# Thresholded attention with a feed-forward block: quarter products added up in their accumulator banks, T2 in the centred tokens' room, and weights turned in place

## Chip, core and metric

The kernel runs on one core of a Trainium2 chip. The metric is the device time of one execution in microseconds (us), as the median of several runs. Engines are named as in the profile: PE is TensorE (matmul), PEld its weight load, DVE VectorE, ACT ScalarE, POOL GpSimd, SP the queue that issues most transfers.

## What is computed

Two stages, all in fp32. First, attention with a threshold for 8 batches of 8 heads, 576 tokens, 64 features per head: scores below their row's maximum less tau are dropped before the softmax. The heads are put side by side to 576 tokens of 512 features. Second, a feed-forward block on them: normalise each token, multiply by w_ch1 (512 x 2048), take the positive part, multiply by w_ch2 (2048 x 512), add the tokens.

```
scores = q @ k.T / 8
scores = where(scores >= rowmax(scores) - tau, scores, -1e9)
a = exp(scores - rowmax);  a = a / (sum(a) + 1e-9);  x = a @ v      # 8 heads -> (8, 576, 512)
xn = (x - mean(x)) / sqrt(var(x) + 1e-6) * g_ln
out = x + maximum(xn @ w_ch1, 0) @ w_ch2
```

## The kernel before

**Attention in slots.** A batch is cut into 9 slots: four pairs of heads with the first 256 queries, one slot with the last 64 queries of all four pairs, and four pairs with the queries 256 to 511. There are 72 slots, n = 0 to 71. In each slot:

- PE writes the scores into two PSUM rooms (L422).
- `exponentials(n)`: DVE takes the negated row maximum (L436), POOL makes the threshold `thr` from it (L440), ACT writes the exponentials into a room `e` in SBUF (L449), four blocks of 128 x 576.
- `weights`: DVE compares with the threshold and masks each block, with its row sum (L458), and takes the reciprocal of each pair of sums (L463). POOL multiplies each block by its reciprocal, "the division" (L474), two blocks as soon as a reciprocal is there.
- `turn_blocks` (from slot n = 6 on): DVE transposes blocks of 32 x 32 out of `e` into a tile `et` (L548, and L542 for the slot with the last queries). SP sends `et` to a room `scr` in DRAM (L555, L559), and fetches it back as `em` and `er` with the keys along the partitions (L569 to L578). So the weights are transposed by a way through DRAM, one slot later.
- `values_of`, two slots later: PE multiplies `em` and `er` by the values (L617, L627), into the same PSUM rooms, and ACT copies the result into the tokens x (L640, L635).

New q and k come by transfer, POOL scales q (L355), and DVE transposes both (kT L373, qT L377 and L382, q_last L383).

**Feed-forward in groups.** The tokens of a batch make two groups of 288, so there are 16 groups, g = 0 to 15. POOL sums the features (L669), PE makes the mean from the sum, DVE centres the tokens into a room `xc` (L692). `first_part(g)` has 64 products of 128 x 288, whose positive parts ACT writes into the room `hidden` (L834). The variance's root comes out as `rb`. The second part of group 0 is plain. From group 1 on, `second_quarters` multiplies by w_ch2 as 2 x 2 blocks with seven products of quarters in place of eight. Each product is a *segment*: 16 calls of `product`, which are 32 matmuls of 64 columns (two records each in the profile). A segment accumulates in one of the two PSUM banks `ff`, in turn, and ACT copies it out (L912). b11, b12, b21 and b22 are the quarters of `hidden` (first or second half of the features; `early` or `late` half of the tokens). Besides segments there are sums of quarters, two halves of 128 x 576 each (L897):

- T3 = b22 - b12 (POOL, into b12); T2 = b11 + T3 (DVE, into b11); T4 = b21 - T2 (POOL, into b21); T1 = b22 - T2 (DVE, into b11)
- S2, S3, S4: differences of weight quarters, made once in group 1
- segments in order: w00·b11, w01·b21, s3·T3, s2·T2, w11·T4, w10·T1, s4·b22
- seven additions of 128 x 2 x 144 of their copies (L937), named u2, 11, u3, 21, 22, u4 and 12; then `finish` multiplies by `rb` (L945) and adds x (L937), and `store` transposes the result into `ot` (L737), which goes to the output.

**What sets the order.** Each engine runs its instructions in the order in which the program emits them; a tile framework adds the waits. The program emits slot by slot, each slot in four quarters. In every quarter `second_part(n, i)` takes steps from the generator of the group at hand, as many products as a share by hand (`ROOM`) says, so that PE always has products between the steps of the attention. The sums of quarters and the additions are not emitted where the generator comes by them: `later` puts them into a list `drops`, with an engine and a cost. Calls of `drip` in the loop over the slots take them from it (the ones marked `urgent` at the next call); `need` emits all of the list up to the ones named, at once. So the place of a sum among the instructions of its engine follows from the quarter in which the generator passed it. After a slot's first quarter those urgent for POOL at the head of the list are emitted as well.

```
def need(*what):
    while not done.issuperset(what):
        drops.pop(0)[-1]()
```

**Weights.** w_ch1 and w_ch2 arrive as raw 64-bit words and are converted in 32 chunks during the first slots, in rooms that are free then (`Weights`: ACT L295 and L300, DVE L310 to L317, POOL L325). One of them is the tile `et`, another is the second `e` room, which after slot 6 is free and later holds S4.

Of the kernel before, what the change touches and what calls it, by code (L numbers as in the profile page):

```python
# [18 lines left out]
def kernel(  # L19
# [87 lines left out]
    hidden = consts.tile([128, ND, TOK], F32, name="hidden")  # L107
    e_room = [consts.tile([128, 4, S], F32, name=f"e{i}") for i in range(2)]

# [84 lines left out]
    class Weights:  # L194
# [13 lines left out]
        def __init__(self):  # L208
# [21 lines left out]
            y_room = ffn.tile([128, NK, TOK], F32, tag="sq", bufs=1, name="y_room")  # L230
            et_room = att.tile([128, NB, 128], F32, tag="et", bufs=1, name="et_room")
            stage = self.stage = consts.tile([128, 8, WC], F32, name="stage")
# [6 lines left out]
            for t, n, before in (  # L239
                (w2_sb.rearrange("p m d c -> p (m d) c"), ND // 2, lambda p: (16, 16, 19, 21, 24, 24, 25, 29)[p]),  # L240
                (hidden, 4, lambda p: 10),
                (x_room, 1, lambda p: 2 * n1),
                (y_room, 1, lambda p: 2 * n1),
                (et_room, 2, lambda p: n1 - 3),
                (stage, 4, lambda p: 2 * n1),
            ):
                for p in range(n):
                    home = 99 if t.shape[-1] != 128 or n != ND // 2 else n1 + 2 * p
                    self.free.append(
                        (before(p), -1, flat(t)[:, p * 2 * WC : (p + 1) * 2 * WC], home)  # L250
                    )

        def take(self, t):
            t = t.rearrange("p a b -> p (a b)")
            for p in range(2):
                self.free.append((2 * self.n1, -1, t[:, p * 2 * WC : (p + 1) * 2 * WC], 99))

# [102 lines left out]
    def turn(u):  # L360
# [7 lines left out]
        if not 0 < u < HP:  # L368
            scale_q(u, q_in)
        qT = att.tile([128, 2, QH], F32, tag="qT", bufs=4, name="qT")  # L370
        kT = att.tile([128, S], F32, tag="kT", bufs=4, name="kT")
        ql = q_last[u % HP]
        nc.vector.transpose(kT, k_in.rearrange("p n c -> p (n c)"))  # L373
        for s in range(2):
            part = q_in[:, 9 * s : 9 * s + 8]
            if by_blocks(units[u][0] * SLOTS + units[u][1] + (HP + 1 if s else 0)):
                nc.vector.transpose(  # L377
                    qT[:, s].rearrange("p (j a c) -> p a j c", j=2, a=4),
                    part.rearrange("p (a j) c -> p a j c", j=2),
                )  # L380
            else:
                nc.vector.transpose(qT[:, s], part.rearrange("p n c -> p (n c)"))  # L382
        nc.vector.transpose(  # L383
# [21 lines left out]
    def scores(b, s):  # L405
# [12 lines left out]
        for t, h, j, at, n, o in sorted(pieces):  # L418
            r = slice(64 * h, 64 * h + 64)
            for i in range(2):  # L420
                qT, kT, ql = turned[b * HP + (2 * j + i if s == HP else hp)]
                nc.tensor.matmul(  # L422
                    sc[h][64 * i : 64 * i + 64, at : at + n],
                    lhsT=ql[r] if s == HP else qT[r, half, j * 128 + 64 * i : j * 128 + 64 * i + 64],
                    rhs=kT[r, o : o + n], start=True, stop=True,
                )

    def exponentials(n):
# [3 lines left out]
        thr = small.tile([128, 4], F32, tag="thr", name="thr")  # L432
        es = e_room[(n + 1) % 2 if n <= FIRST else 0]
        for h in range(2):
# [11 lines left out]
        for i in range(4):  # L446
            if i == 2:
                yield es, thr
            nc.scalar.activation(es[:, i], blocks[i], func=AF.Exp, bias=neg[:, i : i + 1])  # L449

    def weights(n, es, thr, divide):
# [3 lines left out]
        for i in range(4):  # L455
            if i == 3:
                run(n, "mask")
            nc.vector.scalar_tensor_tensor(  # L458
                out=es[:, i], in0=blocks[i], scalar=thr[:, i : i + 1], in1=es[:, i],
                op0=ALU.is_ge, op1=ALU.mult, accum_out=den[:, i : i + 1],  # L460
# [75 lines left out]

    def turn_blocks(b, s, es):


        et = att.tile([128, NB, 128], F32, tag="et", bufs=1, name="et")  # L540
        if s == HP:
            nc.vector.transpose(  # L542
                et.rearrange("p n (u c) -> p u n c", u=HP),
                es.rearrange("p u (n c) -> p u n c", c=32),
            )
        else:
            for h in range(2):
                nc.vector.transpose(  # L548
                    et[:, :, 64 * h : 64 * h + 64].rearrange("p n (j c) -> p j n c", j=2),
                    es[:, 2 * h : 2 * h + 2].rearrange("p j (n c) -> p j n c", c=32),  # L550
                )
        scr = dram.tile([4, S, 128], F32, tag="scr", name="scr")
        if b == 0:
# [6 lines left out]
            out=scr.rearrange("a (r n) x -> (a r) (n x)", r=32),  # L560
            in_=et.rearrange("p n x -> p (n x)"),
        )
# [212 lines left out]
    def differences():  # L775


        flat = conversion.stage.rearrange("p a b -> p (a b)")
        flat4 = e_room[1].rearrange("p a b -> p (a b)")
        size = HM * HD * 128  # L780
        for t in (flat[:, :size], flat[:, size : 2 * size], flat4[:, :size]):
            more.append(t.rearrange("p (m d c) -> p m d c", m=HM, d=HD))
        s2, s3, s4 = more
        s1 = w2[1, 0]
# [12 lines left out]
    def first_part(g):  # L797
# [6 lines left out]
        for d in range(ND):  # L804
# [6 lines left out]
            for c in range(NK):  # L811
# [4 lines left out]
                if c == NK // 2 - 1 and sq is not None and rb is None and (  # L816
# [8 lines left out]
                    if plain:  # L825
                        two = [ffn.tile([128, HM, HT], F32, tag="part", bufs=4, name="two") for _ in two]
                        two = [t.rearrange("p m t -> p (m t)") for t in two]
                    nc.scalar.activation(two[0], var, func=AF.Identity, bias=eps_sb)
# [38 lines left out]
    def second_quarters(g, rb):  # L867
# [9 lines left out]
        part_of = lambda t, i, j: t[:, HM * i : HM * i + HM, (early, late)[j]]  # L877
        y11, y12, y21, y22 = (part_of(y, i, j) for i in range(2) for j in range(2))
        done = set()

# [17 lines left out]

        def segment(weights, rhs, out=None):
            seg = bank(HM, HT)  # L900
            for d in range(HD):
                for m in range(HM):
                    at, end = (d, m), (HD - 1, HM - 1)
                    product(
                        seg[:, m], lhsT=weights[:, m, d], rhs=rhs[:, d],
                        start=at == (0, 0), stop=at == end,
                    )
                    if at != end:
                        yield 2, 0.5
            if out is None:  # L910
                out = ffn.tile([128, HM, HT], F32, tag="part", bufs=4, name="part")
            nc.scalar.copy(out, seg)  # L912
            return out

        def last_tiles(weights, rhs):


            for m in range(HM):
# [8 lines left out]
                drip(everything=True)  # L927
                z = ffn.tile([128, HT], F32, tag="part", bufs=4, name="z")
                dve.tensor_tensor(out=z, in0=end, in1=rb[:, late], op=ALU.mult)
# [9 lines left out]
        def finish(eng, i, j=None):  # L939
# [11 lines left out]
        banks_taken[0] = True  # L951
        yield from segment(w2[0, 0], b11, y11)
        need("t3")
        later(("t2", 3, by_fours, dve, b11, b11, b12, ALU.add), urgent=dve)
        yield 2, 0.5
        p2 = yield from segment(w2[0, 1], b21)
        need("t2")
        later(("t4", 3, by_fours, pool, b21, b21, b11, ALU.subtract), urgent=pool)
        yield 2, 0.5
        p7 = yield from segment(s3, b12)  # L960
        yield 2, 0.5
        yield from segment(s2, b11, y12)
        need("t4")
        later(("t1", 3, by_fours, dve, b11, b22, b11, ALU.subtract), urgent=dve)
        later(
            ("u2", 1, add, pool, y12, y12, y11), ("11", 1, add, pool, y11, y11, p2),
            ("done11", 2, finish, pool, 0, 0),
        )
        yield 2, 0.5
        p4 = yield from segment(w2[1, 1], b21)  # L970
        later(("u3", 1, add, dve, y22, y12, p7), ("21", 1, add, dve, y21, y22, p4))
        if ends_here:
            later(("done21", 2, finish, dve, 1, 0))
        yield 2, 0.5
        need("t1", "u2", "11")
        p5 = yield from segment(w2[1, 0], b11)
        later(("22", 1, add, dve, y22, y22, p5), ("u4", 1, add, dve, y12, y12, p5))
        if ends_here:
# [6 lines left out]
        yield 2, 0.5  # L985
        last = last_tiles(s4, b22) if ends_here else segment(s4, b22)
        for _ in range(12 if g % 2 == 0 else 8):
            yield next(last)
        banks_taken[0] = False
        while waiting_mean:  # L990
            mean_of(waiting_mean.pop(0))
        p3 = yield from last
        if not ends_here:
            later(
                ("12", 1, add, dve, y12, y12, p3), ("done12", 2, finish, pool, 0, 1),
                *((f"o{m}", 1, store, dve, g, m, y[:, m]) for m in (2, 3, 0, 1)),
            )
# [116 lines left out]
    for n in range(NS):  # L1114
# [10 lines left out]
        rest = exponentials(n)  # L1125
        es, thr = next(rest)
        conversion.carry_all()
# [44 lines left out]
        if blocks_go:  # L1172
            conversion.fetch(0 if n == FIRST + 2 else 3, wait=0)
            conversion.prepare_to(end_at, False)
            scr = turn_blocks(b, s, es)
            if n == FIRST:
                conversion.take(e_room[1])
            if n == FIRST:
# [83 lines left out]
```

## Time and profile before

| | us |
|---|---|
| median of 3 runs | 1339.2 (1338.88 to 1339.34) |
| the profiled execution, its own time | 1339.53 |
| its span in the profile | 1337.5 (2.03 lie around it) |
| one batch (two groups, nine slots) in the steady part | 157.28 |
| one segment of 64 records, 128 x 144 | 3.92 |
| L458 mask, DVE, mean of one | 0.810 |
| L474 division, POOL, median and mean of one | 0.747, 0.794 |
| L897 sum of quarters, half of it: POOL mean, DVE mean | 1.426, 0.886 |
| L937 addition: DVE, POOL, median of one with two y operands | 0.457, 0.803 |
| L912 copy, ACT | 0.404 |
| L548 transposes of 1152 elements, DVE, mean of one | 1.376 |
| L542 transposes of 2304 elements, DVE, mean of one | 2.58 |
| scr from et, from issue to landing, median | 5.0 |
| em from scr, from issue to landing, median | 5.7 |

The profile shows one execution. Times in it count from the start of the span. A line of a timeline gives the start, the busy time (of all instances, where it has an x count), engine, source line, operation, the tile written <- those read, shapes, and in brackets how long the engine idled before and what released it. A matmul is "busy" from its issue to a modelled end, so that PE's time says when it had work, not how well it used its array. TensorE's granted clock was 0.998 of full speed.

PE idled before a matmul for 20 us in all in the list of waits; 5.6 of them (3 waits) were for POOL's conversion of weights (L325), 2.6 for the centred tokens, 2.0 for one transfer of em. All but 0.6 us of these end before 180 us, or stand behind 1260 us.

### The profile page before, as it was taken

To read this page: it belongs to the slowest core of one execution; us is meant where nothing else is said; L and a number is where in the kernel's file an instruction comes from. 1 tells how busy PE (TensorE), PEld (TensorE's weight loads), DVE (VectorE), ACT (ScalarE), POOL (GpSimd) and SP (SyncE) were. 2 spreads that over 40 slices of the span, in tenths; PEclk is the share of its full clock that TensorE was granted. 3 is DMA by queue.
4 is the path that set the end of the run, shared out by engine and by line. 5 is a ranking of instruction groups with operands and counts; after the bars stand their busy time and mean duration, and the time that the engine had idled before them with its cause. 6 is when DMAs were issued, how large, how long until landed. Compare 5 with 4: busy or idle time off the path is not lost.

```text
span 1337.5 us, 40245 instructions
## 1 busy us (share of the span) xinstructions
PE 1310.3 (98%) x17304; PEld 996.2 (74%) x17304; DVE 872.5 (65%) x1544; ACT 457.7 (34%) x995; POOL 624.7 (47%) x836
## 2 busy tenths in 40 slices
PE   8899899999999999999999999999999999999997
PEld 7665567769687786968778696877869687786967
DVE  7879886667666675666756677566756667666113
ACT  5866323232423233232233324233232323333120
POOL 3475556535445444445535454443444445345312
PEclk9999999999999999999999999999999999999999
DMA  8946874457543775447734676447754376443211
GB/s 160 293 119 174 206 190 156 179 154 196 176 151 128 191 197 162 152 157 200 191 127 151 171 180 192 139 143 198 196 171 153 133 191 179 139 149 141 73 19 20
DMA packets 335298, 213.92 MB, mean 160 GB/s; under 512 B 247376, under 2 KB 292688, under 8 KB 327056
## 3 DMA queue, kind: packets, MB, share of 16 engines
q1 hardware_dynamic: 329008, 210.46, 54.0%
q8 instruction: 136, 2.23, 0.7%
q10 hardware_dynamic: 5952, 0.74, 0.4%
q0 software_dynamic: 160, 0.15, 0.1%
q14 instruction: 42, 0.34, 0.1%
HBM read 124.00 MB, written 87.29 MB: 158 GB/s over the span
## 4 chain that ended last, share of the span: by engine, by line
PE 91%; ACT 2%; DVE 2%; SPq 2%; DMA 1%; POOL 1%; issue 1%; POOLq 0%; DVEq 0%; ACTq 0%
PE ff L118 70%; PE sc L422 10%; PE sc L617 9%; PE sc L627 2%; SPq L135 1%; ACT e L449 1%; POOL w L325 1%; DVE e L458 1%; DVE xc L692 0%; DMA v_in<-in_v_dram 0%; DVE neg L436 0%; DMA k_in<-in_k_dram 0%; DMA scr<-et 0%; DMA qk_room<-in_k_dram 0%; POOL e L474 0%
## 5 line engine op out<-in xcount | busy, mean ns | idle before, releaser
L118 PE MATMUL ff<-xc,w 128*64 128x288 f32 x4096 | 516.5, 407 | 2.8 <-DVE xc L692 2.0
L118 PEld LDWEIGHTS ff<-xc,w 128*64 128x64 f32 x4096 | 293.5, 137 | 199.9 <-issue 13.9
L436 DVE TENSOR_REDUCE neg<-sc 128x2 f32<-128x1152 f32 x144 | 188.7, 1352 | 269.3 <-PE sc L422 268.7
L118 PE MATMUL ff<-hidden,w 128*64 128x144 f32 (+1 forms) x4096 | 281.2, 294 | 5.7 <-POOL w L325 5.6
L118 PEld LDWEIGHTS ff<-hidden,w 128*64 128x64 f32 x4096 | 252.7, 137 | 31.0 <-issue 9.6
L474 POOL TENSOR_SCALAR e<-e,den 128x576 f32<-128x576 f32 x264 | 206.3, 794 | 141.2 <-DVE den L463 141.2
L458 DVE SCALAR_TENSOR_TENSOR e<-sc,thr,e 128x576 f32<-128x576 f32 x288 | 222.9, 810 | 19.3 <-POOL thr L440 11.7
L440 POOL TENSOR_SCALAR thr<-neg,low_sb 128x2 f32<-128x2 f32 x144 | 39.7, 277 | 378.2 <-DVE neg L436 377.5
L834 ACT ACTIVATE hidden<-ff 128x288 f32<-128x288 f32 x256 | 106.8, 417 | 282.8 <-PE ff L118 278.9
L449 ACT ACTIVATE e<-sc,neg 128x576 f32<-128x576 f32 x288 | 197.8, 754 | 2.6 <-DVE neg L436 2.6
L548 DVE STREAM_TRANSPOSE et<-e 128x1152 f32<-128x1152 f32 x118 | 162.0, 1376 | 16.5 <-POOL e L474 15.9
L422 PE MATMUL sc<-kT,qT 64*64 64x384 f32 (+3 forms) x2048 | 140.2, 403 | 2.0 <-DVE e L458 1.6
L617 PE MATMUL sc<-em,v_in 128*64 128x128 f32 (+1 forms) x2368 | 131.6, 265 | 2.3 <-DMA em<-scr 2.0
L617 PEld LDWEIGHTS sc<-em,v_in 128*64 128x64 f32 x2368 | 124.6, 138 | 10.7 <-DVE den L463 2.2
L118 PE MATMUL ff<-hidden,stage 128*64 128x144 f32 x1920 | 123.3, 286 | 0.0
L118 PEld LDWEIGHTS ff<-hidden,stage 128*64 128x64 f32 x1920 | 117.6, 137 | 2.9 <-issue 2.9
L640 ACT COPY x<-sc 128x128 f32<-128x128 f32 x120 | 31.8, 266 | 245.4 <-PE sc L422 175.7
L897 POOL TENSOR_TENSOR hidden<-hidden 128x576 f32<-128x576 f32 x60 | 84.7, 1426 | 51.7 <-ACT hidden L834 42.1
L422 PEld LDWEIGHTS sc<-kT,qT 64*64 64x64 f32 x2048 | 76.3, 133 | 43.5 <-issue 21.4
L912 ACT COPY part<-ff 128x288 f32<-128x288 f32 x74 | 29.9, 404 | 191.2 <-PE ff L118 190.8
L897 DVE TENSOR_TENSOR hidden<-hidden 128x576 f32<-128x576 f32 x60 | 51.1, 886 | 49.6 <-PE ff L118 46.7
L118 PE MATMUL ff<-hidden,e 128*64 128x144 f32 x960 | 65.5, 286 | 0.0
(126 smaller groups left out, 988.9 us busy)
## 6 DMA issues: line engine op xcount, KB each, us to landing
scr<-et SPq DMA_DIRECT2D x63, 1152.0 KB, 5.0
em<-scr SPq DMA_DIRECT2D x63, 1024.0 KB, 5.7
out_dram<-ot SPq DMA_DIRECT2D x248, 36.0 KB, 3.9
q_in<-in_q_dram SPq DMA_DIRECT2D x120, 72.0 KB, 2.6
er<-scr SPq DMA_DIRECT2D x132, 64.0 KB, 5.1
k_in<-in_k_dram SPq DMA_DIRECT2D x116, 72.0 KB, 2.9
v_in<-in_v_dram SPq DMA_DIRECT2D x28, 256.0 KB, 5.4
w<-in_moe_w_ch_dram SPq DMA_DIRECT2D x10, 512.0 KB, 8.0
```

The lines of the kernel that those rows point to most:

```text
L118: nc.tensor.matmul(out[r], lhsT=lhsT[:, r], rhs=rhs, **flags)
L422: nc.tensor.matmul(sc[h][64 * i : 64 * i + 64, at : at + n], lhsT=ql[r] if s == HP else qT[r, half, j * 128 + 64 * i : j * 128 + 64 * i + 64],
L436: nc.vector.tensor_reduce(out=neg[:, i], in_=pairs[h], axis=AXL.X, op=ALU.max, negate=True,)
L440: nc.gpsimd.tensor_scalar(out=thr[:, i], in0=neg[:, i], scalar1=-1.0, scalar2=low_sb, op0=ALU.mult, op1=ALU.add,)
L449: nc.scalar.activation(es[:, i], blocks[i], func=AF.Exp, bias=neg[:, i : i + 1])
L458: nc.vector.scalar_tensor_tensor(out=es[:, i], in0=blocks[i], scalar=thr[:, i : i + 1], in1=es[:, i], op0=ALU.is_ge, op1=ALU.mult, accum_o ...
L474: nc.gpsimd.tensor_scalar(out=es[:, i], in0=es[:, i], scalar1=den[:, i : i + 1], scalar2=1.0, op0=ALU.mult, op1=ALU.mult,)
L548: nc.vector.transpose(et[:, :, 64 * h : 64 * h + 64].rearrange("p n (j c) -> p j n c", j=2), es[:, 2 * h : 2 * h + 2].rearrange("p j (n c) ...
L617: nc.tensor.matmul(dst[64 * h : 64 * h + 64], lhsT=vt[:, h, c, :], rhs=pick(em[:, 2 * j : 2 * j + 2, c], h), start=c == 0 and first, stop= ...
L640: nc.scalar.copy(x_of(2 * b + (s > HP))[:, s % (HP + 1), 128 * j : 128 * j + 128], pv[j])
L834: nc.scalar.activation(hidden[:, d], p1, func=AF.Relu)
L897: eng.tensor_tensor(out=out[at], in0=in0[at], in1=in1[at], op=op)
```

## The change

The list of segments is put in another order, and products that belong to one result are accumulated on top of each other in a bank, which ACT copies out in between:

- segment 1 is w01·b21, copied to y12; segment 2 is w00·b11 in a bank `one`, copied to y11; segment 3 is s3·T3 in the bank `two`, copied to y22; segment 4 adds s2·T2 into `one`, copied to y21; segment 5 adds w11·T4 into `two`, copied into a part of T2's tile; segment 6 adds w10·T1 into `one`, copied to y12; segment 7 is s4·b22, copied to a tile `rest`.
- The additions 11, 21, 22 and 12 are left; u2, u3 and u4 go.
- T2 has a tile of its own, in the ring of the centred tokens (tag "xc", one room). T1 is still written into b11, T4 into b21.
- T4 waits for T2 by `need` after segment 3; before, after segment 2.
- The tiles `part` go; `rest`, z and two small tiles of group 0 take the tag "o".
- `et` goes. The weights are written with the four blocks interleaved in runs of 32 columns ("p (n i c)"), where they are turned by blocks, and DVE transposes them where they lie, in two calls in every slot. SP sends `scr` from the room itself. Both `e` rooms are used in turn in all slots.
- S4 has a tile of its own, which also stages weights; `et` and the second `e` room do so no longer. qT is split into two tiles, one for each half of the queries (2 and 4 rooms).

```diff
-    e_room = [consts.tile([128, 4, S], F32, name=f"e{i}") for i in range(2)]
+    e_room = [consts.tile([128, 4 * S], F32, name=f"e{i}") for i in range(2)]
+    s4_room = consts.tile([128, NK // 2, ND // 2, 128], F32, name="s4")
+    def by_rows(e):
+        return e.rearrange("p (i s) -> p i s", i=4)
+    def by_columns(e):
+        return e.rearrange("p (n i c) -> p i n c", i=4, c=32)
...
-                (et_room, 2, lambda p: n1 - 3),
+                (s4_room.rearrange("p m d c -> p (m d) c"), 2, lambda p: 2 * n1),
...
-        qT = att.tile([128, 2, QH], F32, tag="qT", bufs=4, name="qT")
+        qT = [att.tile([128, QH], F32, tag=f"qT{i}", bufs=2 + 2 * i, name=f"qT{i}") for i in range(2)]
...
+    def as_in(es, block):
+        return block if len(es.shape) == 3 else block.rearrange("p (n c) -> p n c", c=32)
...
-        es = e_room[(n + 1) % 2 if n <= FIRST else 0]
+        room = e_room[(n + 1) % 2]
+        es = by_columns(room) if by_blocks(n) else by_rows(room)
...
-            nc.scalar.activation(es[:, i], blocks[i], func=AF.Exp, bias=neg[:, i : i + 1])
+            nc.scalar.activation(
+                es[:, i], as_in(es, blocks[i]), func=AF.Exp, bias=neg[:, i : i + 1]
+            )
...
-    def turn_blocks(b, s, es):
-        et = att.tile([128, NB, 128], F32, tag="et", bufs=1, name="et")
-        if s == HP:
-            nc.vector.transpose(
-                et.rearrange("p n (u c) -> p u n c", u=HP),
-                es.rearrange("p u (n c) -> p u n c", c=32),
-            )
-        else:
-            for h in range(2):
-                nc.vector.transpose(
-                    et[:, :, 64 * h : 64 * h + 64].rearrange("p n (j c) -> p j n c", j=2),
-                    es[:, 2 * h : 2 * h + 2].rearrange("p j (n c) -> p j n c", c=32),
-                )
+    def turn_blocks(b, s, room):
+        et = room.rearrange("p (n x) -> p n x", x=128)
+        for h in range(2):
+            two = et[:, :, 64 * h : 64 * h + 64]
+            nc.vector.transpose(two, two)
...
-            in_=et.rearrange("p n x -> p (n x)"),
+            in_=room,
...
+        t2 = ffn.tile([128, NK, TOK], F32, tag="xc", bufs=1, name="t2")
+        t2 = t2.rearrange("p c t -> p (c t)").rearrange("p (d t) -> p d t", d=HD)
...
-        def segment(weights, rhs, out=None):
-            seg = bank(HM, HT)
+        def segment(weights, rhs, out, seg=None):
+            more_of_it = seg is not None
+            if not more_of_it:
+                seg = bank(HM, HT)
...
-                        start=at == (0, 0), stop=at == end,
+                        start=at == (0, 0) and not more_of_it, stop=at == end,
+                        skip_group_check=more_of_it,
...
-            return out
+            return seg
...
-        yield from segment(w2[0, 0], b11, y11)
+        yield from segment(w2[0, 1], b21, y12)
+        later(("t2", 3, by_fours, dve, t2, b11, b12, ALU.add), urgent=dve)
+        yield 2, 0.5
+        one = yield from segment(w2[0, 0], b11, y11)
         need("t3")
-        later(("t2", 3, by_fours, dve, b11, b11, b12, ALU.add), urgent=dve)
         yield 2, 0.5
-        p2 = yield from segment(w2[0, 1], b21)
+        two = yield from segment(s3, b12, y22)
         need("t2")
-        later(("t4", 3, by_fours, pool, b21, b21, b11, ALU.subtract), urgent=pool)
+        later(("t4", 3, by_fours, pool, b21, b21, t2, ALU.subtract), urgent=pool)
+        later(("11", 1, add, pool, y11, y11, y12), ("done11", 2, finish, pool, 0, 0))
         yield 2, 0.5
-        p7 = yield from segment(s3, b12)
+        yield from segment(s2, t2, y21, one)
+        need("t4")
+        later(("t1", 3, by_fours, dve, b11, b22, t2, ALU.subtract), urgent=dve)
         yield 2, 0.5
-        yield from segment(s2, b11, y12)
-        need("t4")
-        later(("t1", 3, by_fours, dve, b11, b22, b11, ALU.subtract), urgent=dve)
-        later(
-            ("u2", 1, add, pool, y12, y12, y11), ("11", 1, add, pool, y11, y11, p2),
-            ("done11", 2, finish, pool, 0, 0),
-        )
-        yield 2, 0.5
-        p4 = yield from segment(w2[1, 1], b21)
-        later(("u3", 1, add, dve, y22, y12, p7), ("21", 1, add, dve, y21, y22, p4))
+        need("t1", "11")
+        yield from segment(w2[1, 1], b21, t2[:, :HM], two)
+        later(("21", 1, add, dve, y21, y21, t2[:, :HM]))
...
-        need("t1", "u2", "11")
-        p5 = yield from segment(w2[1, 0], b11)
-        later(("22", 1, add, dve, y22, y22, p5), ("u4", 1, add, dve, y12, y12, p5))
+        yield from segment(w2[1, 0], b11, y12, one)
+        later(("22", 1, add, dve, y22, y22, y12))
...
-        last = last_tiles(s4, b22) if ends_here else segment(s4, b22)
+        need("21")
+        next_bank(two)
+        rest = ffn.tile([128, HM, HT], F32, tag="o", bufs=4, name="rest")
+        last = last_tiles(s4, b22) if ends_here else segment(s4, b22, rest)
...
-            scr = turn_blocks(b, s, es)
-            if n == FIRST:
-                conversion.take(e_room[1])
+            scr = turn_blocks(b, s, room)
```

## The prediction

> **What bounds the kernel now.** First the page's busy table: it says which engine fills the span.
>
> ```profile
> PE 1310.3 (98%) x17304; PEld 996.2 (74%) x17304; DVE 872.5 (65%) x1544; ACT 457.7 (34%) x995; POOL 624.7 (47%) x836
> ```
>
> TensorE (PE) is busy in 1310.3 of 1337.5 us. The 27.2 us left are not spread out: 20-us windows show 19 us of it before 180 us (while the weights are converted), 0.6 near 254 us, 0.7 near 1270 us and 7.4 us behind PE's last matmul. In between PE never pauses:
>
> ```profile
> 160.00:180.00 20.00, 17.82 (x184) 10.99 (x178) 17.19 (x33) 6.48 (x13) 10.29 (x13) 1.00 0.71 179
> 380.00:400.00 20.00, 20.00 (x368) 18.83 (x364) 13.47 (x19) 4.17 (x9) 10.12 (x13) 1.00 0.52 186
> 537.00:557.00 20.00, 20.00 (x362) 18.83 (x360) 13.75 (x19) 4.17 (x9) 10.40 (x13) 1.00 0.53 182
> 1200.00:1220.00 20.00, 20.00 (x206) 12.89 (x204) 12.77 (x22) 8.26 (x18) 12.04 (x16) 1.00 0.31 120
> ```
>
> (The second number is PE's busy time; the next are its weight loads, DVE, ACT and POOL.) So work taken off DVE, ACT or POOL there gains nothing, while any operand that is late for PE is paid in full: nothing later wins it back. PE's own work is unchanged: the changed program holds the same matmuls in the same interleaving. The forecast is thus a search for operands that come late.
>
> **The late one: T4 in the odd groups.** The second part of a group has seven segments of 32 matmuls (64 records, 3.92 us). Fifth is w11·T4. Before, T4 (POOL, two halves) was emitted ahead of segment 3, two segments before its use. Now it waits for T2 and is emitted behind segment 3, one segment before its use. POOL runs in order, so I laid POOL's list of the changed program beside that of before. In even groups T4 stays behind the slot's four divisions. In groups 3, 5, 7, 9, 11 and 13 it stood ahead of them (thr, sum, thr, T4, four divisions) and now stands behind them. In group 1 it stays ahead. The timeline of before, group 3, PE then POOL then DVE:
>
> ```profile
> 543.93 8.01 PE L118 MATMUL ff<-hidden,stage 128*64 128x144 f32 x128
> 551.77 1.52 PE L118 MATMUL ff<-hidden,w 128*64 128x144 f32 x22
> ```
>
> ```profile
> 546.45 2.81 POOL L897 TENSOR_TENSOR hidden<-hidden 128x576 f32<-128x576 f32 x2
> 549.24 2.92 POOL L474 TENSOR_SCALAR e<-e,den 128x576 f32<-128x576 f32 x4
> ```
>
> ```profile
> 548.12 0.17 DVE L463 RECIPROCAL den<-den 128x2 f32<-128x2 f32 x1
> ...
> 549.80 0.17 DVE L463 RECIPROCAL den<-den 128x2 f32<-128x2 f32 x1
> ```
>
> The 128 "stage" records are segments 3 and 4; segment 5 is due at 551.77. T4 was done at 549.26 and the divisions used the wait. Now the divisions go first, and the second two need the second reciprocal, of 549.80. In the changed list DVE's T1 (L897, two halves) also moves: it followed the transposes and now directly follows that reciprocal. What such a sequence does shows in even groups today, where T2 stands at that place:
>
> ```profile
> 621.52 0.17 DVE L463 RECIPROCAL den<-den 128x2 f32<-128x2 f32 x1
> 621.60 1.41 DVE L897 TENSOR_TENSOR hidden<-hidden 128x576 f32<-128x576 f32 x2
> ```
>
> ```profile
> 620.13 1.47 POOL L474 TENSOR_SCALAR e<-e,den 128x576 f32<-128x576 f32 x2 [2.69 <-DVE den L463]
> 621.78 2.48 POOL L474 TENSOR_SCALAR e<-e,den 128x576 f32<-128x576 f32 x2 [0.19 <-DVE den L463]
> 624.23 2.78 POOL L897 TENSOR_TENSOR hidden<-hidden 128x576 f32<-128x576 f32 x2
> ```
>
> Two divisions take 1.47 us alone and 2.48 beside DVE's addition, and T4's first half starts 624.23 − 621.52 = 2.71 us after the reciprocal. Copied to group 3: 549.80 + 2.71 = 552.51; T4's first half takes 1.40 (2.81/2), so 553.91; PE starts 0.06 after a POOL result (the conversion at 165.08 takes 1.29 and PE restarts at 166.43): 553.97. Due 551.77: PE waits **2.20 us**. The second half is done at 555.30, before PE wants it at 553.97 + 1.96. The other five groups repeat these times (T4 now at 703.73, segment 5 at 709.05; 861.02 and 866.34; 1018.31 and 1023.62; 1175.59 and 1180.91). 6 × 2.20 = **+13.2 us**. Behind T4 on POOL stand the addition 11, its scaling and the residual (3 × 0.8), done by about 558, while POOL's next threshold is due at 562.8: nobody waits. T1 is for segment 6, 3.9 us after segment 5.
>
> The Trainium skill ("SBUF — State Buffer", section "Who interferes with whom") says that a VectorE instruction with two SBUF inputs and a GpSimd instruction that reads SBUF exclude each other, the one that starts first blocking the other wholly. By that the divisions would begin only as DVE's 1.41 us end, and be done some 0.2 us later than in the row of 2.48, so that the total would be about 1 us more; I keep the row.
>
> **The rest, part by part.**
>
> *Three additions fewer per group.* 15 × (one POOL 0.83, two DVE 0.46) lie beside a busy PE: 0. Only in the last group is a chain bare: ACT's copy of segment 6 ends at 1326.63, then two additions of 0.41 each, scaling, z, the last transposes to 1332.12, output to 1337.5. One addition goes: **−0.4**. Next late is PE's last product, 1330.11, against the second z at 1330.99 − 0.41 = 1330.58: still covered.
>
> *Accumulating in the banks.* The two banks alternate as before; the copies (0.40) have the same sizes and each still has a segment of 3.92 us before its bank is written again. 0. Swapping segments 1 and 2: 0. T2 in the room of the centred tokens: the next centring waits for readers that end segments earlier: 0.
>
> *Even groups.* T1 goes ahead of the kT and qT transposes, and addition 11 with its finish (3 × 0.8 us, more beside T1) ahead of q's scaling on POOL. qT and the masks come 1.2 to 1.7 us later; the centring, ended at 646.6, comes to 647.5 to 648.2, due at 649.14; the scores need qT at 647.09, 8 us later. 0, with about 1 us of cover.
>
> *Output transposes (L737) one slot earlier in odd groups.* They await POOL's last sums, to about 581.4, so the reduction due at 580.53 starts at about 582.2. The masks then end near 588.5; PE writes their score banks at 590.66. 0, cover 2 us.
>
> *Turning in place.* Same elements (2 × 1152: 1.38 each; the last-queries slot has 2.76 for 2.58). scr leaves from the weights' room, so that room waits for its transfer (5.0 us), but the two rooms alternate: cover over 10 us. SP's order of scr, em and er is the same. PE took em at 607.98, 7 us after its landing near 600.7; the transposes shift by under 2. 0.
>
> *Rows of 32 with a stride in exponential, mask and division.* No row shows them on POOL. DVE's strided transpose of qT takes 404 ns, the flat one 402: I take 0. Bounds: −0.1 to +0.35 us per division (half of 0.74, the excess that POOL additions show when hindered: 1.07 against 0.80 and up to 1.38). In the T4 chain two count: up to +0.7 × 6 = +4.
>
> *Weight staging.* Chunks 26 and 27 are fetched near 107 to 109 us for 97.87, needed by ACT at 129.2: hidden unless they delay em of slot 7, for which PE already waits 2.0 us near 130. The 4.08 us wait near 150 keeps its cause (POOL's conversions). 0, bounds −2 and +3.
>
> **Sum.** 1339.53 (profiled, span 1337.5 and 2.03 around it) + 13.2 − 0.4 = 1352.3; that run is 0.33 over the median 1339.2, so **1352.0** on the median.
>
> **Rivals.**
> (a) *T4 late, but undisturbed divisions*, if T1's halves miss the divisions. Against: the rows at 621.60, and the same at 236.81. Second two divisions 550.06 to 551.51, T4's first half 552.91, PE 552.97: 1.20 × 6 = 7.2: **1346.0**. 0.14.
> (b) *The strided divisions are slower as well*: up to 2.9 us per group, **1356**. Against: 404 beside 402. 0.12.
> (c) *No late operand, so no slower.* T4's cover decides: PE's 551.77 against the first half's end. If that end came 2.2 us earlier (T4 taken before the divisions, as group 1 has it) only the tail's 0.4 is left: **1338.8**, within 0.2%; with the staging's −2 even below. For it: T4 before had 2.5 us to spare. Against: the order on POOL. 0.08.
> (d) *A cover of 1 us fails too* (centring in even groups, six more waits of about 1): **1358**. 0.06.
> Forecast itself: 0.60.
>
> **Numbers.** 0.2% is 2.7 us, about what a measurement of this kernel can tell from no change. Slower: all but (c): 0.91 (some of (a) and (c) is uncertain by the staging). Same 0.06, faster 0.03. The range reaches from (a) less the staging's 2 to (d), and leaves out (c): 1344 to 1358.
>
> **What would show it.** Right: PE waits for POOL's T4 in six places some 159 us apart, 2.2 us each, at segment 5 of groups 3 to 13; the T4 row behind the divisions; two divisions of 2.5 us beside T1; period 159.5 instead of 157.28; PE full elsewhere. Wrong: PE still full from 380 to 400, a wait on xc or em, or divisions far from 0.74 us.

## The result, and the profile after

The changed kernel takes **1359.76 us** (median of 5 runs, 1358.42 to 1360.77) against 1339.2 (1338.88 to 1341.33) before: 1.015 times as long, 95% interval 1.0135 to 1.0165. The profiled execution has a span of 1357.6 us, 20.1 more than before. The forecast had the sign and the largest term, but 1352.0 for 1359.8, and the time lies 1.8 above the range's end of 1358.

The row of the page's busy table, PE's list of waits and PE's windows come first. The waits: who waited for whom, us in total, times, longest.

```profile
PE 1313.8 (97%) x17304; PEld 998.9 (74%) x17304; DVE 859.5 (63%) x1521; ACT 457.8 (34%) x995; POOL 622.2 (46%) x821
```

```profile
PE ff L127 <- POOL hidden L900: 12.1, 6, 2.0
PE ff L127 <- POOL w L328: 6.0, 4, 4.1
PE ff L127 <- ACT hidden L835: 5.8, 9, 0.7
PE ff L127 <- DVE xc L694: 2.6, 4, 0.7
```

```profile
380.00:400.00 20.00, 17.98 (x298) 16.53 (x294) 13.67 (x19) 4.20 (x10) 11.46 (x13) 1.00 0.46 163
...
540.00:560.00 20.00, 17.98 (x298) 16.54 (x296) 13.95 (x19) 4.49 (x10) 11.46 (x13) 1.00 0.45 156
560.00:580.00 20.00, 20.00 (x322) 16.98 (x320) 11.27 (x21) 6.01 (x14) 6.74 (x14) 1.00 0.34 116
580.00:600.00 20.00, 19.32 (x216) 12.70 (x214) 11.50 (x21) 7.16 (x17) 10.20 (x13) 1.00 0.43 145
```

DVE and POOL do less (13.0 and 2.5 us), PE's instructions are the same 17304, and PE now pauses in two kinds of places: 2.02 us for T4 (L900) in six groups, as foreseen, and 0.68 us behind seven odd groups for ACT's relu (the positive part; L835, L834 before), which was not foreseen. (The other two relu waits of the list, 1.0 us in all, were there before.) Before, such windows were full.

The place of T4 in group 3, in the timelines of PE, POOL and DVE after:

```profile
551.70 4.09 PE L127 MATMUL ff<-t,stage 128*64 128x144 f32 x64
557.81 2.43 PE L127 MATMUL ff<-hidden,w 128*64 128x144 f32 x36 [2.02 <-POOL hidden L900]
```

```profile
552.24 1.47 POOL L484 TENSOR_SCALAR e<-e,den 128x576 f32<-128x576 f32 x2 [1.89 <-DVE den L473]
553.90 2.48 POOL L484 TENSOR_SCALAR e<-e,den 128x576 f32<-128x576 f32 x2 [0.20 <-DVE den L473]
556.35 2.78 POOL L900 TENSOR_TENSOR hidden<-hidden,t 128x576 f32<-128x576 f32 x2
```

```profile
553.64 0.17 DVE L473 RECIPROCAL den<-den 128x2 f32<-128x2 f32 x1
553.73 1.41 DVE L900 TENSOR_TENSOR hidden<-hidden,t 128x576 f32<-128x576 f32 x2
```

T4 starts 556.35 - 553.64 = 2.71 us behind the reciprocal, and the two divisions beside T1 take 2.48: both to the digit what even groups showed before. Segment 4 starts at 551.70 and has 3.92 us of work, so segment 5 was due at 555.62 and started at 557.81: 2.19 late. (The wait's 2.02 is less, since the last matmul's modelled end lies later than its turn.)

The other place, one slot behind group 3, in DVE's, ACT's and PE's timelines:

```profile
587.29 0.84 DVE L739 STREAM_TRANSPOSE ot<-y 128x288 f32<-128x288 f32 x2 [0.80 <-POOL y L941]
588.05 1.32 DVE L444 TENSOR_REDUCE neg<-sc 128x2 f32<-128x1152 f32 x1
```

```profile
589.41 0.27 ACT L642 COPY x<-sc 128x128 f32<-128x128 f32 x1 [2.46 <-DVE neg L444]
589.57 1.38 ACT L457 ACTIVATE e<-sc,neg 128x576 f32<-128x576 f32 x2
590.83 0.42 ACT L835 ACTIVATE hidden<-ff 128x288 f32<-128x288 f32 x1
```

```profile
586.52 4.10 PE L127 MATMUL ff<-xc,w 128*64 128x288 f32 x32
591.30 3.13 PE L127 MATMUL ff<-xc,w 128*64 128x288 f32 x24 [0.68 <-ACT hidden L835]
```

The output transposes wait for POOL's last sums, the row maximum stands behind them on DVE, and on ACT the copy of x and two exponentials wait for the maximum. The relu that empties a bank of PE stands behind the exponentials. PE has two banks; it fills both (32 records, 3.92 us of work) and then waits. The same slot before, in DVE's, PE's and ACT's timelines:

```profile
580.53 2.62 DVE L436 TENSOR_REDUCE neg<-sc 128x2 f32<-128x1152 f32 x2 [5.99 <-PE sc L422]
...
591.55 1.55 DVE L737 STREAM_TRANSPOSE ot<-y 128x288 f32<-128x288 f32 x4
```

```profile
580.43 7.01 PE L118 MATMUL ff<-xc,w 128*64 128x288 f32 x56
```

```profile
583.35 0.42 ACT L834 ACTIVATE hidden<-ff 128x288 f32<-128x288 f32 x1
```

There the output transposes stood 11 us behind the row maximum, and the relu ended at 583.77, 3.34 us after PE had begun to fill the banks: 0.58 us to spare. A relu that comes 1.44 us later is 0.86 too late, and PE goes on 0.05 behind it (590.83 + 0.42, then 591.30): about the 0.92 measured below.

To see where each part of the 20.1 us comes from, I took the start of every slot's row maximum in both traces and subtracted, after less before:

| slots | after - before, us | what lies between |
|---|---|---|
| up to 15 (start, weights converted) | +0.09 | staging of weights: nothing |
| 16 to 17 | +1.55, +1.01 | output transposes of group 1 |
| 20 | +0.85 | an even group: 0.16 gained |
| 24 | +3.10 | T4 of group 3: 2.24 |
| 25 to 26 | +4.54, +4.02 | output transposes: 0.92 |
| 29 | +3.86 | an even group: 0.15 gained |
| 68 to 69 | +15.77, +19.68 | T4 of group 13: 2.24, and 1.67 more |
| 71 | +20.60 | output transposes |
| the span | +20.1 | the last group's chain: 0.5 gained |

The sum: T4 6 x 2.24 = 13.4; output transposes 7 x 0.92 = 6.4; even groups 6 x -0.155 = -0.9; tail -0.5; 1.7 once in group 13. The last one is no wait. The windows behind that pause, with the granted clock in the third column from the right:

```profile
1197.00:1199.00 2.00, 0.12 (x2) 0.13 (x4) 1.86 (x2) 0.30 (x1) 2.00 (x3) 0.99 0.00 0
1199.00:1200.00 1.00, 1.00 (x10) 0.98 (x12) 0.00 (x0) 0.00 (x0) 1.00 (x1) 0.50 0.40 155
...
1202.00:1203.00 1.00, 1.00 (x16) 0.99 (x14) 0.00 (x0) 0.00 (x0) 0.69 (x1) 0.81 0.40 166
1203.00:1204.00 1.00, 1.00 (x20) 1.00 (x18) 0.00 (x0) 0.00 (x0) 0.00 (x0) 1.00 0.07 28
```

After this pause PE was granted half its clock for some 3.4 us. It counts as busy in that time, so neither the busy table nor the waits show it.

### The profile page after: what moved, and what is told of

Read it like the earlier page. It is cut to its first block, busy times and chain, and to the rows that moved or that the text cites. A ratio compares the mean times of both kernels' runs of the same rounds, so it can differ in the third digit from the quotient of the medians.

```text
span 1357.6 us, 40186 instructions
## 1 busy us (share of the span) xinstructions
PE 1313.8 (97%) x17304; PEld 998.9 (74%) x17304; DVE 859.5 (63%) x1521; ACT 457.8 (34%) x995; POOL 622.2 (46%) x821
## 5 line engine op out<-in xcount | busy, mean ns | idle before, releaser
L484 POOL TENSOR_SCALAR e<-e,den 128x576 f32<-128x576 f32 x264 | 213.6, 821 | 151.3 <-DVE den L473 151.3
L448 POOL TENSOR_SCALAR thr<-neg,low_sb 128x2 f32<-128x2 f32 x144 | 45.8, 319 | 392.6 <-DVE neg L444 390.0
L835 ACT ACTIVATE hidden<-ff 128x288 f32<-128x288 f32 x256 | 106.7, 417 | 280.0 <-PE ff L127 278.4
L553 DVE STREAM_TRANSPOSE e<-e 128x1152 f32<-128x1152 f32 x132 | 181.1, 1374 | 12.9 <-POOL e L484 12.2
L916 ACT COPY y<-ff 128x288 f32<-128x288 f32 x75 | 30.5, 407 | 137.3 <-PE ff L127 133.9
L739 DVE STREAM_TRANSPOSE ot<-y 128x288 f32<-128x288 f32 x60 | 25.2, 457 | 77.5 <-POOL y L941 77.4
L127 PE MATMUL ff<-hidden,s 128*64 128x144 f32 x960 | 64.9, 286 | 0.0
L127 PE MATMUL ff<-t,stage 128*64 128x144 f32 x960 | 64.1, 287 | 0.0
L900 POOL TENSOR_TENSOR hidden<-hidden 128x576 f32<-128x576 f32 x30 | 42.7, 1433 | 42.0 <-ACT hidden L835 42.0
L127 PEld LDWEIGHTS ff<-hidden,s 128*64 128x64 f32 x960 | 60.1, 137 | 2.4
```

The source lines that it names most:

```text
L127: nc.tensor.matmul(out[r], lhsT=lhsT[:, r], rhs=rhs, **flags)
L448: nc.gpsimd.tensor_scalar(out=thr[:, i], in0=neg[:, i], scalar1=-1.0, scalar2=low_sb, op0=ALU.mult, op1=ALU.add,)
L484: nc.gpsimd.tensor_scalar(out=es[:, i], in0=es[:, i], scalar1=den[:, i : i + 1], scalar2=1.0, op0=ALU.mult, op1=ALU.mult,)
L553: nc.vector.transpose(two, two)
L835: nc.scalar.activation(hidden[:, d], p1, func=AF.Relu)
L900: eng.tensor_tensor(out=out[at], in0=in0[at], in1=in1[at], op=op)
```

## The experiments

The theory after the traces: two changes of order (T4 behind the divisions, output transposes ahead of the row maximum) are the whole loss, with a half-clock stretch behind some pauses on top; 1.0 of T4's 2.2 us is T1 beside the divisions. Rivals: strides, the accumulation onto a bank that was just copied, or the staging cost something. In the first four runs the kernel before had a median of 1339.21, in the last four 1339.23.

**T4 early** (`e1_t4_early`). The changed kernel, with T4 where it was:

```diff
         need("t3")
+        need("t2")
+        later(("t4", 3, by_fours, pool, b21, b21, t2, ALU.subtract), urgent=pool)
         yield 2, 0.5
         two = yield from segment(s3, b12, y22)
-        need("t2")
-        later(("t4", 3, by_fours, pool, b21, b21, t2, ALU.subtract), urgent=pool)
```

> The changed kernel with T4 (and the need for T2) emitted behind segment 2 again, so that in groups 3 to 13 T4 stands ahead of the four divisions on POOL. Theory (the wait for T4 costs 2.2 us in each of six groups, and one half-clock stretch of 1.7 us follows from one of those pauses): 13.4 + 1.7 go, 1359.8 - 15.1 = about 1344.7 us; PE's list of waits has no POOL L900 left, and keeps some 7 waits of 0.7 for ACT's relu. Rival (divisions with strides, or accumulating onto a bank that was just read, are what costs): above 1350, with PE still waiting in the second part.

Measured: 1344.24 (1344.04 to 1344.38), ratio 1.0035 (1.0021 to 1.0048). PE waits for L900 no more; the relu waits stay (5.7 us, 9). No half-clock stretch between 180 us and PE's last matmul. The T4 theory holds, and its rival falls.

**Output transposes late** (`e2_ot_late`). The changed kernel, with the four transposes of odd groups behind the next slot's turn (`turn_blocks`):

```diff
-                *((f"o{m}", 1, store, dve, g, m, y[:, m]) for m in (2, 3, 0, 1)),
             )
+            outs = [(f"o{m}", 1, store, dve, g, m, y[:, m]) for m in (2, 3, 0, 1)]
+            if g % 2 == 0:
+                later(*outs)
+            else:
+                def behind():
+                    need("done12")
+                    for _, _, fn, *args in outs:
+                        fn(*args)
+                at_quarter(now // QUARTERS + 1, 3, behind)
```

> The changed kernel with the four output transposes of odd groups emitted behind the next slot's turn, as before the change. Theory (they stand on DVE ahead of the row maximum and wait for POOL's last sums; maximum, exponentials and the relu queued behind them on ACT come 1.4 us late, PE waits 0.7 and loses 0.9 in each of seven batches): 1359.8 - 6.4 = about 1353.4 us, no PE wait for L835 near the slot behind odd groups. Rival (the relu waits for something else on ACT, such as the copies from the banks): 1359.8 unchanged.

Measured: 1358.25 (1356.39 to 1358.47), ratio 1.0135 (1.012 to 1.0151): 4.9 above the expectation. The mechanism is as expected: the row maximum of slot 25 comes no later than that of slot 24 (both +3.81; after: +3.10, then +4.54), and PE does not wait for the relu there. What was wrong is the clock: of the six T4 pauses, three were followed by a half-clock stretch in this run (groups 5, 9 and 11), where the changed kernel had one, and an earlier pause near 131 us too (2.4 us for em), which left the run 1.6 late from slot 9 on. 1353.4 + 2 x 1.7 + 1.6 = 1358.4. So a saved wait can be lost again by where the other pauses then fall (the last section works out how).

**Both** (`e3_both`), the two edits at once.

> Both edits at once, T4 early and the output transposes late; the other parts of the change stay. Theory (these two orders are the whole loss): 1339.2 less 0.4 in the last group's chain, less some 0.9 that even groups gained (0.15 in each of six) = about 1337.8 us. Rival (a part of the loss sits elsewhere: staging of the weights, strides, accumulation): 1341 or more.

Measured: 1338.03 (1337.72 to 1339.47, 11 runs), ratio 0.9991 (0.9982 to 1.0000). The windows that had pauses are full again:

```profile
380.00:400.00 20.00, 20.00 (x368) 18.83 (x366) 12.74 (x19) 4.17 (x9) 11.78 (x14) 1.00 0.48 171
540.00:560.00 20.00, 20.00 (x374) 18.24 (x374) 10.08 (x16) 4.57 (x10) 10.39 (x12) 1.00 0.44 143
580.00:600.00 20.00, 20.00 (x206) 12.34 (x204) 14.84 (x24) 8.91 (x21) 5.97 (x11) 1.00 0.49 156
```

Its slots run 0.16 us per even group ahead of before, 0.96 in all at slot 71. Nothing of the loss is left, and the rest of the change is worth about 1 us. That is the best version here, at the limit of what can be told from no change.

**T1 behind the turn** (`e4_t1_behind_turn`). The changed kernel; T4 stays late, but segment 5 is copied to a tile of its own, so that T1 may come later:

```diff
-        need("t1", "11")
-        yield from segment(w2[1, 1], b21, t2[:, :HM], two)
-        later(("21", 1, add, dve, y21, y21, t2[:, :HM]))
+        p5 = ffn.tile([128, HM, HT], F32, tag="o", bufs=4, name="p5")
+        yield from segment(w2[1, 1], b21, p5, two)
+        later(("21", 1, add, dve, y21, y21, p5))
...
+        need("t1", "11")
         yield from segment(w2[1, 0], b11, y12, one)
```

> The changed kernel with segment 5 copied to a tile of its own, so that T1 need not be done before it; T1 then stands behind the transposes in odd groups, as before the change, and no longer beside the second two divisions. T4 stays behind the divisions. Theory (of the 2.2 us per group 1.0 is the divisions' hindrance by T1's additions): two divisions take 1.47 in place of 2.48, PE waits 1.2 a group, 1359.8 - 6.0, less 1.7 if no half-clock stretch falls in, plus 0.9 for even groups = 1353 to 1355 us. Rival (the order alone makes the 2.2, T1 does not matter): 1359.8.

Measured: 1352.92 (1352.79 to 1353.06), ratio 1.01 (1.0086 to 1.0113). POOL's and PE's timeline at group 3:

```profile
553.10 1.47 POOL L484 TENSOR_SCALAR e<-e,den 128x576 f32<-128x576 f32 x2 [0.20 <-DVE den L473]
554.53 3.37 POOL L900 TENSOR_TENSOR hidden<-hidden,t 128x576 f32<-128x576 f32 x2
```

```profile
556.00 3.90 PE L127 MATMUL ff<-hidden,w 128*64 128x144 f32 x60 [1.01 <-POOL hidden L900]
```

Without T1 beside them the divisions take 1.47, and the wait is 1.01 in place of 2.02. No pause in this run was followed by half clock after 180 us. The 0.16 of the even groups is gone as well, so that gain belongs to the earlier T1.

**T4 late in the kernel before** (`e5_before_t4_late`), the one edit alone:

```diff
         p2 = yield from segment(w2[0, 1], b21)
-        need("t2")
-        later(("t4", 3, by_fours, pool, b21, b21, b11, ALU.subtract), urgent=pool)
         yield 2, 0.5
         p7 = yield from segment(s3, b12)
+        need("t2")
+        later(("t4", 3, by_fours, pool, b21, b21, b11, ALU.subtract), urgent=pool)
```

> The kernel before with one edit: T4 is emitted behind segment 3 in place of segment 2. Its segments, additions, rooms and turning stay. T4 then stands behind the four divisions in groups 3 to 13, and T1 behind the transposes as ever. Theory (place of T4 alone, 1.2 us a group without T1's hindrance, pauses too short for a half-clock stretch): 1339.2 + 7.2 = 1346.4 us. Rival (T4's place costs 2.2 also without T1 beside the divisions): 1352.4. Second rival (T4's place matters only with the new segments): 1339.2.

Measured: 1346.63 (1346.48 to 1347.72), ratio 1.0053 (1.0037 to 1.0068); six waits of 1.0 for L897 and 1.24 us per group from slot to slot. The place of T4 costs what it does without any other part of the change.

**Turning, rooms and staging only** (`e6_turning_only`): the changed kernel with the whole second part of the kernel before, of which these are the lines that tell:

```diff
-                        start=at == (0, 0) and not more_of_it, stop=at == end,
+                        start=at == (0, 0), stop=at == end,
...
+            if out is None:
+                out = ffn.tile([128, HM, HT], F32, tag="part", bufs=4, name="part")
...
-        later(("t4", 3, by_fours, pool, b21, b21, t2, ALU.subtract), urgent=pool)
+        later(("t4", 3, by_fours, pool, b21, b21, b11, ALU.subtract), urgent=pool)
+        yield 2, 0.5
+        p7 = yield from segment(s3, b12)
...
-        later(("22", 1, add, dve, y22, y22, y12))
+        later(("22", 1, add, dve, y22, y22, p5), ("u4", 1, add, dve, y12, y12, p5))
```

> The changed kernel with the second part of before (its segments, seven additions and part tiles): what is left of the change is turning in place with strided exponentials, masks and divisions, the two rooms in turn, the split qT and the other staging of weights. Theory (these cost and gain nothing that PE sees): 1339.2 within 1 us. Rival (strides or staging cost): 1342 or more; the other way (no wait on the one et room): 1337 or less.

Measured: 1339.60 (1339.11 to 1342.39, 11 runs), ratio 1.0004 (0.9996 to 1.0013). Its division takes 795 ns (before 794), the mask 810 (810), the exponential 754 (754), a half of the transposes 1375 (1376). No cost of the strides shows, and none of the single `et` room before.

**A longer pause** (`e7_longer_pause`). The changed kernel with two needless additions ahead of T4 in groups 3 to 13:

```diff
+        def behind_two(eng):
+            if 1 < g < NG - 2 and g % 2:
+                spare = ffn.tile([128, TOK], F32, tag="o", bufs=4, name="spare")
+                for _ in range(2):
+                    add(eng, spare.rearrange("p (d t) -> p d t", d=2), t2[:, 0:2], t2[:, 2:4])
+            by_fours(eng, b21, b21, t2, ALU.subtract)
...
-        later(("t4", 3, by_fours, pool, b21, b21, t2, ALU.subtract), urgent=pool)
+        later(("t4", 3, behind_two, pool), urgent=pool)
```

> The changed kernel with two needless POOL additions of 128 x 288 (0.87 us each) ahead of T4 in groups 3 to 13, so that PE pauses 3.7 us in place of 2.0. Theory (the clock falls to half for 3.4 us, at 1.7 us of loss, behind a pause by how it lies to a stretch of fixed length, here all or nearly all of the six, where the 2.0 us pauses had it in 1 of 6 and 3 of 6): 1358.1 + 6 x 1.75 + 5 or 6 x 1.7 = 1377 to 1379 us. Rival (half clock comes by chance whatever the pause): 1368.6 + one or two of 1.7 = 1370 to 1372.

Measured: 1376.13 (1375.78 to 1377.01), ratio 1.0274 (1.026 to 1.0288), 0.9 below the expectation: the waits came to 3.63 each, and five of the six were followed by half clock, 1.67 us lost each time from slot to slot. That of group 5 was not. The rival falls; how a pause must lie to be followed is worked out in the last section.

**Output transposes early in the kernel before** (`e8_before_ot_early`), the other order alone: in odd groups `need("done12")` and the four transposes at the head of the next slot, ahead of its row maximum.

```diff
-                *((f"o{m}", 1, store, dve, g, m, y[:, m]) for m in (2, 3, 0, 1)),
...
+                def ahead():
+                    need("done12")
+                    for _, _, fn, *args in outs:
+                        fn(*args)
+                at_quarter(now // QUARTERS + 1, -3, ahead)
```

> The kernel before with one edit: the output transposes of odd groups and the last POOL sums that they need are emitted ahead of the next slot's row maximum. Theory (maximum, exponentials and relu come late, PE loses 0.9 in each of seven batches): 1339.2 + 6.4 = 1345.6 us, with a PE wait on L834 of 0.7. Rival (the relu's lateness belongs to the new segments): 1339.2.

Measured: 1362.33 (1362.15 to 1364.01), ratio 1.0173 (1.0159 to 1.0187): the sign is right, but 23.1 us are lost where 6.4 were expected. PE waits 2.57 to 2.62 us for the relu behind each of the seven odd groups (with two short waits 19.1 us in all, 9 times) and loses 2.82 a batch. In the kernel before POOL has y11's scaling and residual in the same stretch (2 x 0.80), so the last sums come 1.9 us later than in the changed kernel, counted from the scores, and I had taken over the 0.9. In group 3's next slot POOL's last sum starts at 589.65 with scores at 585.76; after the change it was 586.46 with 584.47. The 1.9 us are also what the wait grew by (2.58 in place of 0.68). Two half-clock stretches add 3.4: 7 x 2.82 + 3.4 = 23.1.

## Why the prediction was right in sign and short in size

- **T4 in the odd groups, +13.2**: right. 2.24 a group measured (13.4), with each part of it as derived: 2.71 from reciprocal to T4, 1.40 for its first half. That T1 hinders the divisions was read from rows of even groups; `e4` shows it by its absence, and rival (a), 1.2 a group, is what comes then (`e4` and `e5`: 1.01 of wait, 1.23 to 1.25 from slot to slot).
- **What two SBUF inputs do.** The Trainium skill's rule ("SBUF — State Buffer", section "Who interferes with whom") would have put the divisions' end 0.2 us later than the row of 2.48, by the prediction's estimate; the row came back at 2.48, so the measurement stands.
- **"Output transposes (L737) one slot earlier in odd groups ... 0, cover 2 us": wrong.** This is the step that failed. The reduction's delay was about right (1.7 us forecast, 1.44 measured), but I followed it only through the masks to the score banks. Between them stand ACT's exponentials, and behind these in ACT's order the relu that empties a bank of the first part. The cover there was 0.58 us, not 2. PE waits for that 0.68 us and loses 0.92 in each of seven batches, 6.4 us in all: `e2` removes it, `e8` makes it in the kernel before. The sign "PE full elsewhere" failed with it.
- **The clock**: not in the forecast at all. A pause of 2 us was priced at its length. Half clock took 1.7 us more once in the profiled run of the changed kernel, and 5.1 behind the T4 pauses of `e2`.
- **Even groups, "0, with about 1 us of cover"**: the cover held, and there was a gain of 0.16 that I did not see. In before the 128 records of segments 5 and 6 of group 4 took 8.17 us, in after 8.01: segment 6 was waiting a little for T1, whose first half ended at 636.46 while PE's next weight load came at 636.57, and a merged row hides it.
- **The tail, -0.4**: 0.5 measured. **Strides, turning and staging, 0**: right (`e6`, +0.4 within its interval). **Accumulating in the banks, 0**: right, since `e3` has it and loses nothing.
- With the three missed terms (transposes, clock, even groups) the forecast would have been 1352.0 + 6.4 + 1.7 - 0.9 = 1359.2, against 1359.8 for the median and 1359.4 for the profiled execution, in which the 1.7 was seen. Of rivals (b), (c) and (d) none happened; (d) asked for another failing cover, which there was, but not in the centring.

## What to carry to other kernels

When the engine that bounds is full, an edit that removes work beside it gains nothing, and one that moves work in another engine's order can lose at once: lay the instruction lists of every engine side by side, and for each instruction that comes later follow *all* that stands behind it, on its own engine and on those that wait for it, until you reach the full engine. Covers must be sought in each of these chains; I stopped at the first. A pause of the full engine can cost more than its length: here 1.7 us more behind 4 of 12 pauses of 2 us. Where an addition with two inputs is moved beside another engine's work, look for a row in which the two already meet.

## What the runs showed of the hardware

**Half clock behind short pauses.** Of the 12 T4 pauses with a wait of 2.02 us (after and `e2`) 4 were followed by about 3.4 us at a granted clock of 0.50, 1.7 us lost each; of the 7 relu pauses of 2.57 to 2.62 us in `e8` 2; of 6 with 3.63 us (`e7`) 5; of 12 with 1.0 us (`e4`, `e5`) none. The loss is in PE's busy time, to be seen only in the clock's column. For executions that were timed without a profile only the mean granted clock is on record. It fits: in `e2` the fastest run (1356.39) has 0.994, the other three 0.991 to 0.992.

Which pauses are followed can be read from the traces. In each of the ten the granted clock changes on a grid of its own: all its falls and rises lie whole multiples of 3.413 us apart. After the change it falls at 154.49 and 1198.96 us, 306 steps apart, as short windows on either side show:

```profile
154.38:154.48 0.10, 0.10 (x6) 0.10 (x4) 0.10 (x1) 0.10 (x1) 0.10 (x1) 1.00 1.25 319
154.49:154.59 0.10, 0.10 (x6) 0.10 (x4) 0.10 (x1) 0.01 (x1) 0.10 (x1) 0.50 1.19 271
...
1198.86:1198.96 0.10, 0.08 (x2) 0.09 (x4) 0.00 (x1) 0.00 (x0) 0.10 (x1) 1.00 0.00 0
1198.97:1199.07 0.10, 0.10 (x2) 0.10 (x4) 0.00 (x0) 0.00 (x0) 0.10 (x1) 0.50 0.00 0
```

I cut the 37 pauses above along this grid. The 11 that were followed by half clock left PE idle for 2.02 to 3.32 us of one step; the 26 others for at most 1.95 us of any step. So the pause of group 13 after the change lies wholly in one step (2.02), while a border cuts those of groups 3 to 11 (1.33 to 1.95 in the larger part), and in `e7` that of group 5 is cut into 1.76 and 1.87. Why the limit lies near 2 us no run here tells.

The Trainium skill ("TensorE: Matmul & The Clock Gate", sections "What's actually happening" and "Why this matters for your kernels") gives a free-running window of 3413 ns, by whose activity the clock is set, and advises against gaps over some 3 us. The length of the stretches (3.4 us) and the fixed step agree. The advice does not: gaps of 2.0 us were enough in a third of the cases here.

**Additions of DVE beside divisions of POOL.** The pair of divisions took 1.47 us beside masks or transposes and 2.48 beside a DVE addition with both inputs in SBUF, which itself took 1.41 for its two halves. In these rows DVE began 0.17 to 0.18 us earlier, and POOL paid. In `e4`, where T1 meets T4 in place of the divisions, both paid: T4's two halves took 3.37 (2.78 after the change), T1's 2.62.
